# Attention and MLP layer: a weight scale for each half of w1, the first batch's MLP by halves of the weights, its first stage on four heads at a time, and its steps placed by times

## The chip, the cores and the metric

The kernel runs on one core of a Trainium2 chip. The metric is the device time of one execution in microseconds (us). A core has a matrix engine (TensorE, PE in the profile, with its weight loads as PEld), a vector engine (VectorE, DVE), an activation engine (ScalarE, ACT), a general engine (GpSimd, POOL) and a queue that issues the transfers (SyncE, SP). Each works through its own list of instructions in order and waits on semaphores for the others.

## The reference

Three pieces are computed in a row for 8 batches of 576 tokens and 512 columns (8 heads of 64).

```python
# stage 1: attention through a memory of 32 rows for each head
a = softmax(phi, axis=2)                       # [b, h, 576, 32]
k_m, v_m = a^T k, a^T v                        # [b, h, 32, 64]
x = softmax(q k_m^T / 8) v_m                   # heads side by side: [b, 576, 512]
# MLP with a mix over tokens of rank 32
u = x + ((x^T U) V)^T
y = u + relu(u @ w_ch1) @ w_ch2                # 512 -> 2048 -> 512
# stage 2: top 2 of 4 experts, each a causal attention with one head of 64
w = softmax over the two largest of y @ w_gate
out = sum over e of w_e * softmax(mask(q_e k_e^T / 8)) v_e @ wo[e]
```

The weights w_ch1, w_ch2, U and V come as float64, everything else as float32.

## The kernel before

**Numbers.** A float64 weight is read as two 32-bit words and turned into float32 by `conv64`: two passes on ACT, three on DVE (of which one, L337, takes the largest absolute value along), one addition on POOL. Then `split` writes it as two f16 parts, high and low, times a power of two that makes the largest value fit; the high part and, for some chunks, the scaled float32 are made on ACT, the low part on DVE (`L384`) or POOL (`L378`, `L380`). A matrix product is three f16 products: high by high, high by low, low by high.

**w1 and w2.** w1 is 8 chunks (`w1_load`, `w1_conv`, `w1_split`; 1 MB of words each, in 4 transfers of 256 KB), w2 too (`w2_load`, `w2_conv`, `w2_split`; 1 MB each). The words of w1 are put into the room of `w1s`, the tile that the f16 parts will have later; the float32 goes into the room of `w2s`. There is one scale for all of w1, so `w1_scale` needs all eight conversions, and the first split follows it. w2 has a scale for each chunk.

**MLP.** For each batch and each half of its tokens (288), `up` makes 16 tiles of 128 of the 2048 columns (12 matmuls of 128x288 each, `L999`), ACT and DVE make `h` of each (`L1003`, `L1005`), and `down` sums 8 of them into 4 tiles `dn` (24 matmuls, `L1015`), once for each half of the columns (`fg`). In the order of the program both halves `fg` of the first token half come before the second token half. `u_split` makes the f16 parts `uhl` of the input from `u` and its scale `us`.

**Stage 1** of a batch works on pairs of heads: `pair_kv` makes k_m and v_m (in the first batch in float32, with `L742`), `pair_kb` divides by the sums and puts the two heads apart (`own` is a mask), `pair_qT` transposes q (a transpose for one head, `L775`, and a matmul with the identity for the other, `L776`), `pair_scores`, `soft_a` and `soft_b` make the softmax, and for each half of the heads `half_p`, `half_t`, `half_tt`, `half_tx` and `half_u` make x and the token mix (tiles `at`, `tu`, `tt`, `tx`, `txs`, `u`). `u_max` and `u_scale` follow. Stage 2 (`y_`, `proj`, `vg`, `unit_`) of a batch and stage 1 of the next stand beside the MLP of the one between.

**Order.** Within an engine instructions run in the order in which they are traced, or as the tile scheduler reorders them. The set-up of the weights, batch 0's stage 1 and MLP and batch 1's stage 1 are traced in the order of a table, `ORDER`, written out step by step. From batch 1's MLP on, steps are taken from a heap by times in units of an `up` tile (`at`), and the last two stages follow a table `ORDER2`.

Of the kernel before, what the change touches and what calls it, by code (L numbers as in the profile page):

```python
# [46 lines left out]

ORDER = """  # L50
phi_load.0.0 phi_load.0.1 phi_max.0 phi_max.0 uv_load u_setup v_setup v_setup v_setup u_setup u_setup v_setup
phi_max.0 w1_load.0 w1_conv.0 w1_conv.0 phi_max.0 phi_max.0 raw_load.0.0.0 phi_sub.0.0 phi_sub.0.1 phi_sub.0.0 raw_load.0.0.1 v_setup w1_conv.0
w1_conv.0 phi_sub.0.1 pair_kv.0.0 w1_load.1 w1_load.2 w1_conv.1 w1_conv.1 w1_conv.1 pair_kb.0.0 raw_load.0.0.2
pair_qT.0.0 raw_load.0.1.0 raw_load.0.1.1 w1_conv.2 pair_kb.0.0 pair_kb.0.0 pair_kb.0.0 pair_qT.0.0 w1_conv.1
pair_kb.0.0 pair_kv.0.1 raw_load.0.1.2 raw_load.0.2.0 raw_load.0.2.1 u_setup pair_scores.0.0 w1_conv.0 w1_load.3
w1_load.4 pair_kb.0.1 pair_kb.0.1 pair_kb.0.1 pair_kb.0.1 pair_qT.0.1 pair_qT.0.1 pair_kb.0.1 soft_a.0.0 soft_a.0.0
w1_conv.2 w1_conv.2 pair_kv.0.2 pair_scores.0.1 raw_load.0.2.2 raw_load.0.3.0 pair_qT.0.2 raw_load.0.3.1
raw_load.0.3.2 pair_kv.0.3 soft_a.0.0 w1_conv.3 soft_b.0.0 soft_b.0.0 w2_load.0 w2_load.2 w1_conv.2 w1_conv.4
soft_b.0.0 soft_b.0.0 w1_conv.1 w1_conv.3 w1_load.5 w1_conv.3 pair_kb.0.2 pair_qT.0.2 pair_kb.0.2 pair_kb.0.2
w1_conv.2 w1_load.6 soft_a.0.1 pair_kb.0.2 soft_a.0.1 soft_a.0.1 pair_kb.0.2 v_setup w1_conv.4 pair_qT.0.3  # L60
pair_qT.0.3 soft_b.0.1 pair_kb.0.3 soft_b.0.1 pair_kb.0.3 w2_conv.0 soft_b.0.1 soft_b.0.1 pair_scores.0.2
pair_kb.0.3 pair_kb.0.3 half_p.0.0 w1_conv.3 pair_kb.0.3 soft_a.0.2 soft_a.0.2 soft_a.0.2 half_t.0.0 half_t.0.0
half_p.0.0 half_tt.0.0 w2_conv.0 half_tt.0.0 soft_b.0.2 w1_conv.4 half_tx.0.0 w2_conv.2 w1_conv.3 w1_load.7
soft_b.0.2 half_tx.0.0 soft_b.0.2 soft_b.0.2 w2_conv.0 half_tx.0.0 w2_conv.0 pair_scores.0.3 soft_a.0.3 half_tx.0.0
w1_conv.5 w2_conv.2 soft_a.0.3 soft_a.0.3 w2_conv.2 phi_load.1.0 half_u.0.0.0 half_u.0.0.0 w1_conv.6 soft_b.0.3
half_u.0.0.1 soft_b.0.3 soft_b.0.3 soft_b.0.3 half_p.0.1 half_u.0.0.1 w2_conv.2 w1_conv.4 w1_conv.5 w1_conv.7
half_t.0.1 half_p.0.1 half_tt.0.1 w1_conv.5 half_tt.0.1 half_tx.0.1 w1_conv.6 half_tx.0.1 phi_load.1.1 w1_conv.4
half_t.0.1 w1_conv.6 half_tx.0.1 w1_conv.5 w1_conv.7 w1_conv.7 half_tx.0.1 half_u.0.1.0 half_u.0.0.0 w1_scale
w1_conv.5 w2_conv.2 w2_conv.0 w2_conv.0 w1_conv.6 half_u.0.1.0 w2_load.4 w2_load.6 w2_conv.4 w1_scale w1_scale
half_u.0.1.0 w1_scale half_u.0.0.1 half_u.0.1.1 half_u.0.1.1 half_u.0.1.1 w1_conv.6 u_max.0 w1_split.0 w1_split.0  # L70
u_max.0 u_scale.0 w1_split.1 w1_split.2 w2_conv.2 w2_conv.0 w1_split.1 w1_split.1 u_scale.0 u_split.0.0 w2_conv.4
w2_conv.4 u_split.0.0 w1_split.3 w2_conv.4 w1_conv.7 w2_conv.0 w1_split.4 w1_split.5 w2_conv.2 w2_conv.2 up.0.0
w1_split.2 w2_split.0 w2_split.0 w2_conv.4 phi_max.1 up.0.0 up.0.0 w2_split.2 w2_conv.6 w2_split.2 up.0.1 up.0.2
up.0.1 up.0.1 w1_conv.7 w1_split.6 w2_conv.6 w2_conv.4 up.0.2 w1_split.7 up.0.2 w2_conv.6 up.0.3 up.0.4 up.0.5
up.0.3 w2_conv.4 up.0.3 w1_split.3 w1_split.4 w2_conv.4 w2_load.1 w1_split.3 u_scale.0 w2_conv.1 phi_max.1 up.0.4
up.0.4 phi_max.1 up.0.6 up.0.5 phi_max.1 w2_conv.6 up.0.5 w2_split.4 phi_max.1 phi_sub.1.0 up.0.6 w2_conv.1 w2_conv.1 w2_conv.6 up.0.7 up.0.7
up.0.6 up.0.7 phi_sub.1.0 w2_split.4 w2_load.3 w1_split.5 w2_conv.3 w2_conv.6 w2_conv.1 w2_conv.6 w2_conv.6
w1_split.6 w2_split.6 w2_conv.1 down.0.0.0.0 down.0.0.0.1 down.0.0.1.0 w2_conv.3 w2_conv.3 w2_load.5 phi_sub.1.1
phi_sub.1.1 w1_split.7 w2_conv.1 down.0.0.1.1 down.0.0.0.1 w2_conv.1 w2_conv.1 down.0.0.2.0 w2_split.1 phi_split.1.0
w2_conv.3 w2_split.1 w2_split.1 w2_conv.3 w2_split.6 down.0.0.2.1 down.0.0.3.0 down.0.0.2.1 w2_conv.3 down.0.0.1.1  # L80
phi_split.1.1 w2_conv.3 w2_conv.3 w1_split.5 w2_load.7 w2_conv.5 w2_conv.5 w2_conv.7 down.0.0.3.1 raw_load.1.0.0
down.0.0.3.1 w2_conv.5 up.0.8 up.0.8 up.0.9 up.0.10 up.0.8 w2_conv.7 w2_split.3 w1_split.7 up.0.9 up.0.9 up.0.10
up.0.10 w2_split.3 w2_conv.7 w2_conv.5 raw_load.1.0.1 raw_load.1.0.2 pair_max.1.0 pair_max.1.0 up.0.11 up.0.12
up.0.13 up.0.11 up.0.11 pair_scale.1.0 pair_scale.1.0 w2_conv.7 pair_scale.1.0 w2_conv.5 up.0.12 up.0.12 w2_conv.5
w2_conv.5 up.0.13 pair_hl.1.0.0 phi_split.1.1 up.0.13 up.0.14 up.0.15 up.0.14 up.0.14 w2_conv.7 w2_conv.7 up.0.15
# [1425 lines left out]
```

## Time and profile before

| what | value |
|---|---|
| runs, us | 1393.03 (median), 1390.7, 1398.51 |
| profiled execution, us | 1399.22 |
| its span, first to last instruction, us | 1397.2 |
| mean granted clock of TensorE | 0.970 |
| PE busy, us (share of the span) | 1270.1 (91%) |
| DVE busy | 969.3 (69%) |
| ACT busy | 787.4 (56%) |
| POOL busy | 405.8 (29%) |

An engine's busy time is the sum of its instructions' durations. The granted clock is the share of full speed at which the chip let TensorE run: 1.00 is 2.4 GHz, 0.50 is 1.2 GHz. The profiled execution is one more execution than the three timed ones.

### The profile page before, as it was taken

Reading aid. Unit: us, or ns where it says so; the run is one execution under the profiler, and the core shown is the slowest. Engines: PE = TensorE matmul, PEld = TensorE weight load, DVE = VectorE, ACT = ScalarE, POOL = GpSimd, SP = SyncE. Lnnn points to the kernel's source line nnn. Section 1 sums busy time; section 2 is a strip of 40 time slices with the busy share of each in tenths; the row PEclk is TensorE's granted clock in tenths of the full one; section 3 lists DMA queues with packets and bytes.
Section 4 is the critical chain, followed back from the end, with each engine's and each line's share of the span. In section 5 each row is a group of like instructions: output and inputs, shape, how many; then the busy total and the mean of one; then the engine's idle time right before and its main releaser. Section 6 shows DMA issues by size and latency. Waiting matters only on the chain. (4 is left out here: it accounts for less than half of the span.)

```text
span 1397.2 us, 31201 instructions
## 1 busy us (share of the span) xinstructions
PE 1270.1 (91%) x12021; PEld 973.9 (70%) x12021; DVE 969.3 (69%) x2669; ACT 787.4 (56%) x1888; POOL 405.8 (29%) x381
## 2 busy tenths in 40 slices
...
GB/s 286 206 91 30 132 89 33 10 65 86 95 69 44 83 64 77 70 52 93 76 73 56 80 64 78 70 48 91 75 69 41 95 65 53 57 13 33 42 81 110
DMA packets 253957, 106.42 MB, mean 76 GB/s; under 512 B 199056, under 2 KB 245328, under 8 KB 253808
## 3 DMA queue, kind: packets, MB, share of 16 engines
...
## 5 line engine op out<-in xcount | busy, mean ns | idle before, releaser
L999 PE MATMUL up<-uhl,w1s 128*128 128x288 f16 x3072 | 429.7, 293 | 40.1 <-DVE h L1005 34.8
L1015 PE MATMUL dn<-h,w2s 128*128 128x288 f16 x3072 | 409.9, 287 | 8.3 <-DVE h L1005 8.3
L999 PEld LDWEIGHTS <-w1s 128*128 128x128 f16 x3072 | 301.7, 100 | 133.5 <-issue 49.0
L1015 PEld LDWEIGHTS <-w2s 128*128 128x128 f16 x3072 | 295.0, 98 | 87.8 <-issue 11.7
L1237 POOL TENSOR_TENSOR phl<-pr,phl 128x128 f16<-128x128 f32 (+3 forms) x112 | 92.5, 826 | 331.0 <-ACT phl L1235 234.3
L1005 DVE SCALAR_TENSOR_TENSOR h<-up,h 128x288 f16<-128x288 f32 x256 | 113.0, 449 | 74.5 <-ACT h L1003 73.9
L1003 ACT ACTIVATE h<-up 128x288 f16<-128x288 f32 x256 | 100.8, 402 | 78.0 <-PE up L999 76.7
L1234 ACT ACTIVATE pr<-sc,nm 128x128 f32<-128x128 f32 (+3 forms) x112 | 58.7, 524 | 125.7 <-DVE nm L1228 69.8
L672 POOL TENSOR_TENSOR kvq<-raw,kvq 96x768 f16<-96x768 f32 x48 | 78.4, 1651 | 144.7 <-ACT raw L666 141.4
L633 DVE TENSOR_REDUCE amax<-raw 96x1 f32<-96x768 f32 x72 | 68.0, 946 | 67.8 <-DMA raw<-in_v_dram 31.2
L1022 DVE SCALAR_TENSOR_TENSOR u<-dn,us,u 128x288 f32<-128x288 f32 x128 | 65.3, 511 | 40.2 <-PE dn L1015 39.6
L1298 PEld LDWEIGHTS <-pT 128*128 128x128 f16 (+1 forms) x1260 | 56.2, 102 | 33.5 <-DMA pT<-phl 15.1
L1298 PE MATMUL av<-vhl,pT 128*128 128x64 f16 (+1 forms) x1260 | 68.0, 195 | 11.2 <-DMA pT<-phl 9.3
L1228 DVE CUSTOM_DVE_ANT_0 sc<-sc,wmask,ysc 128x128 f32<-128x128 f32 (+3 forms) x128 | 69.3, 550 | 12.1 <-PE sc L1225 11.1
L660 ACT ACTIVATE kvq<-raw,ps 96x768 f16<-96x768 f32 x72 | 62.6, 924 | 6.6 <-DVE ps L315 6.5
L1235 ACT ACTIVATE phl<-pr 128x128 f16<-128x128 f32 (+3 forms) x112 | 52.2, 466 | 13.9 <-DMA pT<-phl 12.0
L1334 ACT ACTIVATE ohl<-av,fac 128x64 f16<-128x64 f32 (+1 forms) x140 | 35.7, 307 | 41.1 <-PE av L1298 30.6
L1355 PE MATMUL wo<-wos,oT 128*128 128x512 f16 (+1 forms) x288 | 57.1, 348 | 1.2 <-ACT oT L1327 0.7
L1152 PE MATMUL vg<-wvg,yhl 128*128 128x260 f16 (+1 forms) x504 | 48.6, 256 | 0.0
L1104 PE MATMUL pj<-yhl,wqs 128*128 128x288 f16 x336 | 46.2, 286 | 0.7 <-ACT u L909 0.7
L1104 PE MATMUL pj<-yhl,wks 128*128 128x288 f16 x336 | 46.6, 286 | 0.0
L1119 ACT ACTIVATE qst<-pj 64x288 f16<-64x288 f32 x56 | 22.6, 404 | 40.6 <-PE pj L1104 40.1
...
## 6 DMA issues: line engine op xcount, KB each, us to landing
...
raw<-in_k_dram SPq DMA_DIRECT2D x48, 144.0 KB, 2.7
raw<-in_v_dram SPq DMA_DIRECT2D x48, 144.0 KB, 2.7
raw<-in_q_dram SPq DMA_DIRECT2D x48, 144.0 KB, 2.4
...
rx<-in_k_dram SPq DMA_DIRECT2D x16, 144.0 KB, 3.7
```

What stands on the lines that cost most here:

```text
L633: dve.tensor_reduce(o, raw, axis=AX.XYZ, op=ALU.max, apply_absolute_value=True)
L660: act.activation(hl[:, 0], src, AF.Copy, scale=s[0:SP, j:j + 1])
L672: pool.tensor_tensor(hl[:, 1], src, hl[:, 0], op=ALU.subtract)
L999: pe.matmul(pm, w1s[:, f // 2, a, kc, f % 2 * P:f % 2 * P + P], uhl[:, c, kc], start=(n == 0), stop=(n == 3 * KC - 1))
L1003: act.activation(hb[:, 0, g], pm, AF.Relu)
L1005: dve.scalar_tensor_tensor(hb[:, 1, g], pm, 0.0, hb[:, 0, g], op0=ALU.max, op1=ALU.subtract)
L1015: pe.matmul(pm, w2s[:, m, fg, a, g], hb[:, c, g], start=(g == 0 and a + c == 0), stop=(g == FG - 1 and a == 1))
L1022: dve.scalar_tensor_tensor(y, pm, st["us", b][:, 4 + KC * fg + m:5 + KC * fg + m], y, op0=ALU.mult, op1=ALU.add)
L1104: pe.matmul(pp[:, 0:NH], w[:, a, kc, ep * P:(ep + 1) * P], yhl[:, c, kc, ts_], start=(n == 0), stop=(n == 3 * KC - 1))
L1228: dve.tensor_tensor_reduce(psc[:, 0:n], psc[:, 0:n], wmask[:, (NT - 2 - i) * P:(NT - 1) * P], cs, 3.0e38, ALU.add, ALU.min, nm)
L1237: (dve if tail and TD >> (2*i + eo) & 1 else pool).tensor_tensor(phl[:, n:2 * n], pr[:, 0:n], phl[:, 0:n], op=ALU.subtract)
L1298: pe.matmul(pav[:n, eo * D:(eo + 1) * D], lhs, vhl[:kn, c, j, vs], start=(j == 0 and a + c == 0), stop=(j == i and a == 1))
```

## The change

The diff has four parts, shown here cut to their core.

First, w1 gets a scale for each half of its chunks, and the room for words and float32 is given out so that chunks 0 to 3 can be split before chunks 4 to 7 have been converted:

```diff
-    sw1 = cpool.tile([P, 2], F32, name="sw1")
+    sw1 = cpool.tile([P, 4], F32, name="sw1")
+    def slot(c):
+        return c if c < 4 else 2 + c % 2
+    def w1z(c):
+        return w2v[:, 2 * (c % 4) + c // 4]
     def w1_conv(c):
-        z = w2v[:, c]
-        yield from conv64(z, w1v[:, c % W1S].rearrange("p (n t) -> p n t", t=2), part[:, 0, c:c + 1], RP1 >> c & 1)
+        z = w1z(c)
+        yield from conv64(z, w1v[:, slot(c)].rearrange("p (n t) -> p n t", t=2), part[:, 0, c:c + 1], RP1 >> c & 1)
-    def w1_scale():
+    def w1_scale(g):
...
     def w1_split(c):
         yield from split(w1s[:, c, 0].rearrange("p k n -> p (k n)"), w1s[:, c, 1].rearrange("p k n -> p (k n)"),
-              w2v[:, c], sw1[:, 0:1], SP1 >> 2 * c & 3)
+              w1z(c), sw1[:, c // 4 * 2:c // 4 * 2 + 1], SP1 >> 2 * c & 3)
```

Second, batch 0's MLP goes through the first half of the columns for both token halves and then through the second; its `uhl` of the second token half gets tiles of its own:

```diff
-        for h_ in range(2):
-            for fg in range(2):
+        for x in range(4):
+            h_, fg = (x % 2, x // 2) if b == 0 else (x // 2, x % 2)
```

Third, `pair_kv` and `pair_kb` of batch 0 become steps on four heads, and q of batch 0 is loaded so that both heads of a pair lie side by side and are transposed together:

```diff
-                pe.matmul(pk[o:o + 64, n * P:n * P + (P if x is not None else 1)], e[:, c, 64 * p:64 * p + 64],
-                              x[:, :, c] if x is not None else one, start=(c == 0), stop=(c == C - 1))
+            for c in range(C):
+                for g in range(4):
+                    kv = st["rx", b, 2 * hf + g // 2][0:SP, 0:2]
+                    pe.matmul(pk[32 * g:32 * g + 32, 0:P], e[:, c, 4 * hf + g], kv[:, :, g % 2, c], start=(c == 0), stop=(c == C - 1))
...
-                pe.transpose(qp[c // R][0:64, t], raw[:, 0, c], ident[:SP, :SP])
-                pe.matmul(qp[c // R][64:128, t], raw[:, 1, c], ident[:SP, :SP], start=True, stop=True)
+                pe.transpose(qp[c // R][:, c % R * SP:c % R * SP + SP], raw[:, c].rearrange("p h d -> p (h d)"), ident[:SP, :SP])
...
+            for a in range(NA):
+                for h in range(2):
+                    nc.sync.dma_start(t[:, a * R:(a + 1) * R, h],
+                                      src[b, 2 * p + h, a * NH:(a + 1) * NH].rearrange("(p r) d -> p r d", r=R))
```

Fourth, the table `ORDER` goes, and its steps get times in the same heap as the later ones. Steps that only fill (`fill=True`) are pinned on DVE and ACT behind a main step of an earlier time:

```diff
+START, SLACK, SLACK2, LATER = 62, 2.5, 5, 5
...
+                for e in main:
+                    before_ = [i for t_, i in main[e] if t_ <= t - (SLACK if t < T0 else SLACK2) / UNIT]
+                    if pin and fill and before_:
+                        pins.enter_context(tc.issue_after(before_[-1]))
...
+    UNIT = 1.45
+    T0 = START / UNIT
+        at((10, 16, 22, 29)[c] / UNIT, w1_conv, c, fill=True)
+        at((42 + 2 * c) / UNIT, w1_split, c, fill=True)
+    at(38 / UNIT, w1_scale, 0, fill=True)
+    for n, (f, a) in enumerate(mlp(0)):
+        at(T0 + n, f, *a)
+        at(T0 + (4, 7, 11, 15)[c], w1_conv, 4 + c, fill=True)
+        at(T0 + 22 + 2 * c, w1_split, 4 + c, fill=True)
+    at(T0 + 20, w1_scale, 1, fill=True)
+    for t, f, a in stage1(1):
+        at(T0 + LATER + t, f, *a, fill=True)
+        at(T0 + 61 + w, sw_split, w, fill=True)
```

On DVE, shortly ahead of batch 0's first `up`, the program before has this (`w1mx` is the maximum over rows for w1's one scale, `sw_128` that scale, `um` and `ur` the maxima of `u` for the scale of `uhl`):

```order
L410 TENSOR_REDUCE part<-w1mx 128x1
L315 TENSOR_SCALAR sw_129<-t_117 128x1
L313 TENSOR_SCALAR sw_128<-part 128x1
L911 TENSOR_REDUCE um<-u_579 128x1
L317 TENSOR_SCALAR t_117<-t_117 128x1
L315 TENSOR_SCALAR sw_128<-sw_128 128x1
L317 TENSOR_SCALAR sw_128<-sw_128 128x1
L384 SCALAR_TENSOR_TENSOR w1s<-w2s,sw_128,w1s 128x1024 x4
L911 TENSOR_REDUCE um<-u_579 128x1
L915 TENSOR_REDUCE um<-um 128x1
L384 SCALAR_TENSOR_TENSOR w2s<-w2z_480,sw_129,w2s 128x1024
```

At the same place the changed program has this (its line numbers are its own: L320 stands for L384 of before, L242 for L306, L381 for L438, L820 and L828 for L857 and L865, L874 for L911, and on PE L992 for L999 and L1008 for L1015; `w2z` are w2's chunks in float32, `tt`, `ttf`, `th`, `txs` the token mix of the second half of batch 0's heads):

```order
L253 TENSOR_SCALAR t_117<-t_117 128x1
L320 SCALAR_TENSOR_TENSOR w1s<-w2s,sw_128,w1s 128x1024
L242 TENSOR_SCALAR dg<-identb,part 128x128
L874 TENSOR_REDUCE um<-u_539 128x1
L381 TENSOR_REDUCE mx<-w2mx_564 128x1
L874 TENSOR_REDUCE um<-u_539 128x1
L249 TENSOR_SCALAR t_117<-mx 128x1
L820 COPY tt<-tu_1_576 96x128
L251 TENSOR_SCALAR sw_129<-t_117 128x1
L320 SCALAR_TENSOR_TENSOR w1s<-w2s,sw_128,w1s 128x1024
L253 TENSOR_SCALAR t_117<-t_117 128x1
L828 TENSOR_TENSOR ttf<-tt_1_604,halves 128x64
```

The four splits of w1 on DVE in one row became two, apart from each other, with steps of stage 1 and of w2 between them; there are no conversions of w1 beyond chunk 3 above this place.

On PE, amid batch 0's MLP, the changed program has this between the tiles `dn_0_1_0` and `dn_0_1_1` (`tu`, `tt`, `tx` and `u` are the token mix of batch 1's first half of heads, `ar` and `w2mx` maxima for scales; 18 rows of `u` are left out):

```order
L1008 MATMUL dn_0_1_0_1877<-h_0_8_1554,w2s 128x288
L817 MATMUL tu_0_1538<-at,Uf 32x128 x6
L825 MATMUL tt_0_1552<-id_92,tt 128x32
L244 LDWEIGHTS onesb
L244 MATMUL ar_2_1573<-dg,onesb 128x3x96
L244 LDWEIGHTS onesb
L244 MATMUL w2mx_1578<-dg,onesb 128x128
L837 MATMUL tx_0_1587<-vtf,ttf 32x128 x2
...
L869 MATMUL u_1_0_1675<-V_113,txs 128x288
L869 MATMUL u_1_1_1676<-V_113,txs 128x288
L1008 LDWEIGHTS w2s
L1008 MATMUL dn_0_1_1_1915<-h_0_8_1554,w2s 128x288
```

Before, the same chain was spread: `tu`, `tt` and `tx` stand more than a hundred rows apart, and `tx`, for one, stands among `up` and `ss` (scores):

```order
L999 LDWEIGHTS w1s
L999 MATMUL up_1_9_2161<-uhl_1_1514,w1s 128x288
L874 MATMUL tx_0_1950<-vtf,ttf 32x128 x2
L719 LDWEIGHTS qT
L719 MATMUL ss_2_1999<-kb,qT 96x64
```

What moved is the rest of the MLP: in the changed program none of it stands between the steps of the chain.

On PE, at the end of batch 0's MLP, the program before has this (`u_2` and `u_3` are the second half of batch 1's heads; 20 more matmuls of `dn_1_1_3` follow before `ur`):

```order
L1015 LDWEIGHTS w2s
L1015 MATMUL dn_1_1_3_2459<-h_1_8_2147,w2s 128x288
L906 MATMUL u_2_0_2314<-V_113,txs 128x288
L906 MATMUL u_2_1_2315<-V_113,txs 128x288
L906 MATMUL u_3_0_2324<-V_113,txs 128x288
L901 LDWEIGHTS vth
L901 MATMUL u_3_1_2325<-aT,vth 128x288
L901 LDWEIGHTS vth
L901 MATMUL u_3_1_2325<-aT,vth 128x288
L906 MATMUL u_3_1_2325<-V_113,txs 128x288
L1015 LDWEIGHTS w2s
L1015 MATMUL dn_1_1_3_2459<-h_1_8_2147,w2s 128x288
```

The changed program has the whole chain of the second half behind the last row of `dn_1_1_3` (17 rows of `u` are left out):

```order
L1008 MATMUL dn_1_1_3_2407<-h_1_8_2071,w2s 128x288
L825 MATMUL tt_1_2187<-id_92,tt 128x32
L837 MATMUL tx_1_2208<-vtf,ttf 32x128 x2
...
L864 MATMUL u_3_1_2268<-aT,vth 128x288
L869 MATMUL u_3_1_2268<-V_113,txs 128x288
L244 LDWEIGHTS onesb
L244 MATMUL ur_2315<-dg,onesb 128x128
L244 LDWEIGHTS onesb
L244 MATMUL swmx_2376<-dg,onesb 128x384
L244 LDWEIGHTS onesb
L244 MATMUL swmx_2381<-dg,onesb 128x256
L992 LDWEIGHTS w1s
```

The `dn` rows that stood within and behind the chain now stand ahead of it. From the first `up` of batch 1 on, the two programs' rows are nearly the same.

## Rows read from the trace of the kernel before

**Rows 1.** Windows by stage; columns: busy us (instructions), granted clock, DMA, GB/s.
```profile
0.00:120.36 120.36, 75.34 (x352) 56.93 (x353) 88.70 (x155) 60.16 (x88) 55.73 (x46) 0.86 0.59 169
120.36:262.35 141.99, 120.82 (x1080) 92.88 (x1078) 111.06 (x248) 81.15 (x143) 50.78 (x32) 0.94 0.28 72
262.35:420.00 157.65, 153.56 (x1525) 119.09 (x1525) 117.58 (x331) 91.70 (x228) 47.50 (x46) 0.99 0.31 70
```

**Rows 2.** DVE's groups by form, 0 to 120.36 us.
```profile
L343 DVE SCALAR_TENSOR_TENSOR w2s<-w1s,w2s 128x1024 uint32<-128x1024 uint32 x8 | 11.8, 1475 | 0.0
L337 DVE TENSOR_SCALAR_CACHE_REDUCE w2s<-w2s 128x1024 f32<-128x1024 f32 x8 | 9.7, 1208 | 0.1
L384 DVE SCALAR_TENSOR_TENSOR w1s<-w2s,sw,w1s 128x1024 f16<-128x1024 f32 x4 | 9.6, 2437 | 2.1 <-ACT w1s L382 2.1
L343 DVE SCALAR_TENSOR_TENSOR w2z<-w2r,w2z 128x1024 uint32<-128x1024 uint32 x4 | 8.9, 2216 | 0.0
L339 DVE TENSOR_SCALAR w2s<-w2s 128x1024 uint32<-128x1024 uint32 x8 | 8.2, 1019 | 0.1
```

**Rows 3.** PE's groups by form, 0 to 120.36 us.
```profile
L742 PE MATMUL kv<-rx,e 96*64 96x128 f32 x96 | 21.7, 422 | 4.5 <-ACT e L587 4.5
L776 PE MATMUL qt<-ident,rx 96*64 96x96 f32 x48 | 14.0, 394 | 0.0
...
L775 PE MATMUL qt<-ident,rx 96*64 96x96 f32 x24 | 8.9, 369 | 0.0
...
L742 PE MATMUL kv<-one,e 96*64 96x1 f32 x48 | 5.5, 242 | 0.0
...
L794 PE MATMUL at<-ident,at 96*128 96x96 f32 x12 | 2.4, 376 | 0.0
L854 PE MATMUL tu<-at,Uf 96*32 96x128 f32 x24 | 2.2, 421 | 3.1 <-POOL at L829 3.1
```

**Rows 4.** Waits, 0 to 120.36 us: total us, times, longest.
```profile
ACT qT L780 <- PE qt L776: 22.7, 8, 5.7
...
DVE iv L751 <- PE kv L742: 14.6, 2, 7.7
```

**Rows 5.** Timeline about batch 0's first up (start, us; in brackets idle before).
```profile
119.82 1.21 DVE L343 SCALAR_TENSOR_TENSOR w2z<-w2r,w2z 128x1024 uint32<-128x1024 uint32 x1
...
121.08 1.40 DVE L975 SCALAR_TENSOR_TENSOR uhl<-u,us,uhl 128x1152 f16<-128x1152 f32 x1
...
122.53 7.13 PE L999 MATMUL up<-uhl,w1s 128*128 128x288 f16 x33 [1.25 <-DVE uhl L975]
...
136.08 1.63 PE L999 MATMUL up<-uhl,w1s 128*128 128x288 f16 x12 [1.30 <-DVE sw L315]
```

**Rows 6.** Windows of 10 us (columns as in group 1).
```profile
100.00:110.00 10.00, 0.96 (x3) 0.48 (x2) 7.89 (x5) 9.90 (x11) 7.69 (x4) 0.50 0.00 0
120.00:130.00 10.00, 8.75 (x43) 5.60 (x44) 9.57 (x19) 6.17 (x9) 3.56 (x1) 0.57 0.14 45
130.00:140.00 10.00, 6.35 (x50) 4.67 (x49) 9.93 (x11) 7.79 (x14) 9.41 (x4) 1.00 0.17 60
170.00:180.00 10.00, 5.45 (x32) 3.57 (x31) 9.28 (x14) 7.61 (x13) 5.01 (x4) 0.83 0.54 116
```

**Rows 7.** Timeline ahead of batch 1's first up.
```profile
250.89 0.41 PE L874 MATMUL tx<-vtf,ttf 128*32 128x128 f32 x4
...
251.98 4.21 PE L1015 MATMUL dn<-h,w2s 128*128 128x288 f16 x33
...
256.82 2.75 PE L1015 MATMUL dn<-h,w2s 128*128 128x288 f16 x21
...
262.35 0.53 PE L999 MATMUL up<-uhl,w1s 128*128 128x288 f16 x3 [0.72 <-ACT uhl L973]
```

**Rows 8.** DMA issues of the span: count, KB, median us to landing.
```profile
raw<-in_q_dram SPq DMA_DIRECT2D x48, 144.0 KB, 2.4
...
sw<-in_moe_wq_dram SPq DMA_DIRECT2D x4, 128.0 KB, 2.9
```

More of the change, by code (lines that the diff above doesn't have):

```diff
@@ L39 @@
 SP2 = 1028
-W1S = 4
 RB = 3
@@ L55 @@
[L55 to L59, printed above, removed]
@@ L75 @@
[L75 to L79, printed above, removed]
@@ L80 @@
[L80 to L84, printed above, removed]
@@ L948, in stage1 @@
                 hf = p // 2
-                add(t0 + 10.4, half_t if b else half_t_first, hf)
+                add(t0 + 10.4, half_t, hf)
                 add(t0 + 10.5, half_p, hf)
```

298 lines of the change are left out of this document (157 added, 141 removed).

## The prediction

> **What bounds the kernel now.** I read the stretches first. The page puts PE busy for 91% of the span, but that is an average over two different kernels. From batch 1's first `up` tile on, PE works 153.56 of 157.65 us [rows 1] and nothing in the change can win much there. Before it lie two stretches that are not full: the set-up with batch 0's stage 1 (0 to 120.36 us, PE 75.34, DVE 88.70), and batch 0's MLP beside batch 1's stage 1 (141.99 us, PE 120.82, so 21 us idle). The change touches these two alone. In the order of instructions, everything from batch 1's first `up` tile on stands almost as it stood; so the time moves by as much as that tile moves, now at 262.35 us [rows 7].
>
> The first stretch is a stretch of DVE: PE does almost nothing from 100 to 110 us (0.96 us busy) while DVE has 7.89 and ACT 9.90 [rows 6]. The groups of DVE [rows 2] show what it does: conversions of the double-word weights and their splits. The first `up` needs chunk 0 of w1 alone, but its scale needs all eight. The waits add that DVE stood 14.6 us for the `kv` matmuls of stage 1, and ACT 22.7 for `qt` [rows 4].
>
> **The change, part by part.**
>
> *1. A scale for each half of w1.* One w1 chunk costs DVE 1.208 + 1.019 + 1.475 = 3.70 us [rows 2]. Four chunks leave the stretch: -14.8 us. So do two of its four DVE splits: 2 x 2.437 = -4.9. Two more splits of w2 come in ahead, at some 1.3 us each (the 1.40 us of `uhl`'s low half, 1152 columns [rows 5], scaled to 1024 columns: 1.25): +2.6. The low half of `uhl`, now ahead: +1.4 [rows 5]. Two more w2 scales and the wider `kb` steps are short instructions that no group shows; I set them at +1.5 and -0.8. DVE ahead of the first `up`: 88.7 - 14.8 - 4.9 + 2.6 + 1.5 + 1.4 - 0.8 = 74 us.
>
> *2. Stage 1 on four heads at a time.* `kv` is 96 matmuls with 64 output rows in 21.7 us, 0.226 each (and 48 for the sums, 5.5) [rows 3]. After the change they are 96 of 32 rows, each head against its own 128 columns of k and v, and 24 for the sums. The nearest form with 32 rows, `tu`, takes 2.2 us for 24, 0.09 each: 8.7 + 2.7 = 11.4 us where 27.2 stood (if the 0.226 holds, 24). `qt` is 72 instructions of 22.9 us [rows 3] and becomes 24 transposes, which at the 0.2 us of `at` (2.4 us for 12) make 5. These are 34 us of PE work less, in a stretch in which PE is not full: it counts only where someone waits, DVE's 14.6 us [rows 4] above all. I take that as gone.
>
> *3. When does the first `up` start?* DVE is idle 120.36 - 88.7 = 31.7 us before. Without the 14.6 that is 17, and 74 + 17 = 91. GpSimd's share also falls (four conversions and four splits fewer), and with it the stretching of DVE: the same L343 takes 2.216 us on average [rows 2], and 1.21 when nothing runs beside it [rows 5]. Some 3 us of that come back: 88. Bounds: 78, if DVE idles no more than 4 us; 100, if DVE's share stays at 88.7/120.36 = 74%, as 74/0.74.
>
> A rule speaks against it. q of batch 0 comes in 16 loads of 256-byte pieces instead of 8 with longer ones. The whole trace has 128 KB in 256-byte pieces (`sw` of wq) landing in 2.9 us, and 144 KB of q in 2.4 [rows 8]: 1.36 times as long per byte. By these rows 1.18 MB of q cost 1.18/0.128 x 2.9 - 1.18/0.144 x 2.4 = 7 us of landing, laid over each other, and so 2 at most on the path; it is inside the 78 to 100. The Trainium skill (DMA: Bandwidth & Descriptors, Specifications) wants pieces of at least 512 bytes for the line rate; by it these loads would count about double, an estimate of 4 us of a full queue at the 169/0.59 = 286 GB/s of a busy queue [rows 1]. The trace agrees in direction, by 1.36 and not by 2.
>
> *4. Batch 0's MLP by halves of the weights.* What left the first stretch comes back here. DVE: 111.06 + 14.8 + 3.5 (two splits, at less contention than before) - 4 (one and a half w2 conversions, done earlier) - 2.6 (two w2 splits) - 1.4 (`uhl`) - 5.3 (the splits of `sw`, now behind batch 1's first `uhl`) - 1.5 = 115 us; ACT rises too, from 81.15 of 141.99. PE keeps its 121. The first two quarters are `up` and `down` of both token halves with chunks 0 to 3, so the chunks 4 to 7 have two quarters, some 2 x 33 us (16 items of 1.63 us each [rows 5], and a share of the idle time), to be loaded, converted and split. The table of times puts the last conversion 15 and the last split 28 steps of 1.45 us behind the MLP's start, 22 and 41 us; with a conversion and a split of delay (3.7 + 2.4) the last chunk is ready at 47. `up` 8 comes after 32 items, at about 66. Hidden by PE's two quarters, with 19 us to spare; beyond that each us late is a us lost.
>
> PE's idle time here is what decides. (a) 8 us as before, spread (of the 21 before, those in the windows 120 to 140 and 170 to 180 [rows 6] are about half). (b) 3 us at the start (the first `up` waits for the low half of `uhl`, 1.25 before [rows 5]). (c) In the order, batch 1's chain for its first half of heads (`tu`, `tt`, `tx`, `u`) stands back to back between two `dn` tiles, where before `dn` matmuls were spread among them. Its bare latencies are about 5 us; DVE has conversions of 1.0 to 2.2 us between its steps, so I take 12 (5 to 20). (d) At the end the same chain of the second half stands behind the last `dn`. Before, it ran from 250.89 (`tx`) to 262.35 with 33 and 21 `dn` matmuls, 4.21 + 2.75 us, in its gaps [rows 7]. Without these PE has 2 to 3 us of work in 12.5 (the 11.46 and a us from `tt` to `tx`): 10 idle. Sum: 121 + 8 + 3 + 12 + 10 = 154 us against 141.99. Bounds: 142 (the pockets are filled by moving everything else up) and 170 (DVE at 115/170 = 68%, less than in either stretch).
>
> *5. The splits of `sw`* stand on DVE and ACT between batch 1's first `uhl` and its first `h`: four on DVE of 1.25 us (as above), 5 us, of which the `up` tiles already free to run cover most: +2 (0 to 5).
>
> **Sum.** Batch 1's first `up` at 88 + 154 + 2 = 244, against 262.35: 18 us. The profiled execution took 1399.22 us; its like would take 1381. The median of the runs is 6.2 us lower than that execution, so 1393.03 - 18 = 1375.
>
> **The rivals.** *A: the second stretch grows not at all.* For: PE idles 21 us in it and DVE is at 78%; 115 us of DVE at 78% make 147. Against: the order of (c) and (d). With 142, a first `up` at 84, and 2 for the `sw` splits it gives 228: 34 us, 1359.
>
> *B: the gain is given back.* The first `up` comes at 100 since DVE's share stays 74%, and the second stretch takes 160 because the second half of w1 is late: the margin of 19 us goes if each of the four conversions and splits takes half as long again beside `h` and `u` on DVE (9.28 to 9.93 of 10 us busy at 120 to 140 and at 170 to 180 [rows 6]). 100 + 160 + 2 = 262: no change, 1393.
>
> *C: slower, by the clock.* PE's granted clock is 0.50 of full from 100 to 110 and still 0.57 from 120 to 130, with PE 8.75 us busy there: after the idle stretch it worked a while at the lower level, 1.2 GHz. The pockets (c) and (d) could each bring that. 25 us of PE work in each following piece at half speed cost 12.5 more: 88 + 154 + 2 + 25 = 269, 1400. It decides from there: about 25 us beyond the forecast's sum. For it: 0.83 at 170 to 180 with PE 5.45 busy. Against: at 130 to 140 PE has 6.35 busy and the clock is 1.00 [rows 6], so such pockets alone need not lower it.
>
> *D: the change doesn't do what it says* on `kv`: if the 32-column matmuls cost 0.226 each, PE keeps 13 us and DVE half of its 14.6 us wait; the first `up` at 95, 1382, inside the forecast's own range.
>
> **How the numbers follow.** A measurement of this kernel can tell about 0.5%, 7 us, from no change. Forecast (gain of 8 to 30 us, D in it): 0.60. A: 0.15. B: 0.14. C: 0.11. Faster is forecast and A: 0.75; same is B: 0.14; slower is C: 0.11. The time is that of the forecast, 1375, its own range 1363 to 1386: 6 us to either side for the first `up`, and 5 or 6 for the two pockets. The range for 8 in 10 reaches 1353 (A with 78 for the first `up`: 78 + 142 + 2 = 222, 40 us) to 1397 (B and a little); what is left out is C and small parts of A and B.
>
> **What would show it.** In the profile after: the first `up` near 88 us, with four conversions of w1 ahead of it; DVE's wait for `kv` gone, and the 32-column `kv` near 0.09 us; PE idle in one pocket amid `dn_0_1` and one after the last `dn` of batch 0, about 10 us each; batch 1's first `up` near 244; nothing moved behind it by more than 2 us. I am wrong if the first `up` comes after 100, if `up` 8 of the first token half waits for w1, if the clock is at its lower level beyond the first `up` for more than 20 us, or if the stretches behind batch 1's first `up` change.

## The result

The changed kernel took 1379.32 us (median of 4 runs, 1378.6 to 1382.06), the kernel before 1395.77 (4 runs, 1390.7 to 1400.68): a ratio of 0.9886, 95% interval 0.9843 to 0.9929. In a later set of runs it took 1378.04 (4 runs) beside 1390.92 (13 runs): 0.9896, 0.9859 to 0.9934. So it is faster by about 1%, 13 to 16 us. 1375 had been predicted, and the range of 1353 to 1397 holds the time.

The windows by stage, of the changed kernel, cut at the first `up` of batch 0 and of batch 1 (against [rows 1]):

```profile
0.00:88.19 88.19, 43.07 (x277) 33.14 (x278) 65.52 (x142) 48.34 (x77) 37.96 (x37) 0.89 0.71 204
88.19:238.67 150.48, 125.26 (x1077) 95.36 (x1076) 120.13 (x249) 87.50 (x148) 63.95 (x38) 0.89 0.32 84
238.67:396.30 157.63, 151.40 (x1489) 117.00 (x1489) 122.62 (x340) 94.97 (x230) 44.98 (x45) 0.98 0.33 70
```

The first `up` came at 88.19 us (120.36 before, 88 predicted), batch 1's at 238.67 (262.35 before, 244 predicted). What lies behind it took 1376.7 - 238.67 = 1138.0 us of the span, 1134.9 before. So the traces say 23.7 us won and 3.2 given back; but a second trace of the changed kernel has 1141.1 us behind that point, so 3 us there is what one kernel differs by from execution to execution. The runs say 13 to 16 in all, since the profiled execution of before (1399.22 us) was one of its slower ones and that of the changed kernel (1378.6) its fastest.

DVE's groups of the first stretch (against [rows 2]; L279 is L343 of before, L320 is L384, L275 is L339):

```profile
L279 DVE SCALAR_TENSOR_TENSOR w2z<-w2r,w2z 128x1024 uint32<-128x1024 uint32 x4 | 5.0, 1256 | 0.0
...
L279 DVE SCALAR_TENSOR_TENSOR w2s<-w1s,w2s 128x1024 uint32<-128x1024 uint32 x4 | 4.9, 1223 | 0.0
...
L320 DVE SCALAR_TENSOR_TENSOR w1s<-w2s,sw,w1s 128x1024 f16<-128x1024 f32 x2 | 2.9, 1464 | 0.4 <-ACT w1s L318 0.4
L275 DVE TENSOR_SCALAR w2s<-w2s 128x1024 uint32<-128x1024 uint32 x4 | 2.9, 722 | 0.1
```

An L279 on w2's chunks takes 1.256 us where it took 2.216, a split of w1 1.464 where it took 2.437. PE's groups of the same stretch (against [rows 3]):

```profile
L695 PE MATMUL kv<-rx,e 96*32 96x128 f32 x96 | 6.8, 419 | 9.4 <-DMA rx<-in_v_dram 7.0 <-ACT e L539 2.3
L698 PE MATMUL kv<-one,e 96*128 96x1 f32 x24 | 5.4, 354 | 0.0
...
L739 PE MATMUL qt<-ident,rx 96*128 96x96 f32 x24 | 4.7, 373 | 0.0
```

96 `kv` matmuls with 32 rows take 6.8 us, 0.071 each (0.226 before, 0.09 estimated). The 24 for the sums take 5.4, 0.225 each: twice what I took, and no less than the 48 of before (5.5). The 24 transposes of q take 4.7. `kv` now waits 7.0 us for loads of v, which it did not before.

### The profile page after: what moved, and what is told of

It reads as the page before. It is cut to its first block, busy times and chain, and to the rows that moved or that the text cites. A ratio compares the mean times of both kernels' runs of the same rounds, so it can differ in the third digit from the quotient of the medians.

```text
span 1376.7 us, 31068 instructions
## 1 busy us (share of the span) xinstructions
PE 1241.8 (90%) x11948; PEld 952.8 (69%) x11948; DVE 964.3 (70%) x2671; ACT 786.8 (57%) x1886; POOL 401.7 (29%) x379
## 5 line engine op out<-in xcount | busy, mean ns | idle before, releaser
L992 PE MATMUL up<-uhl,w1s 128*128 128x288 f16 x3072 | 425.1, 291 | 35.6 <-DVE h L998 30.3
L1008 PE MATMUL dn<-h,w2s 128*128 128x288 f16 x3072 | 416.4, 289 | 4.7 <-DVE h L998 4.1
L992 PEld LDWEIGHTS <-w1s 128*128 128x128 f16 x3072 | 299.3, 99 | 125.8 <-issue 44.5
L1008 PEld LDWEIGHTS <-w2s 128*128 128x128 f16 x3072 | 297.0, 99 | 89.6 <-issue 8.5
L1015 DVE SCALAR_TENSOR_TENSOR u<-dn,us,u 128x288 f32<-128x288 f32 x128 | 64.9, 509 | 33.3 <-PE dn L1008 32.7
L1292 PEld LDWEIGHTS <-pT 128*128 128x128 f16 (+1 forms) x1260 | 56.3, 102 | 41.3 <-DMA pT<-phl 23.7
L1113 ACT ACTIVATE qst<-pj 64x288 f16<-64x288 f32 x56 | 22.7, 406 | 42.1 <-PE pj L1098 41.7
```

What stands on the lines that cost most here:

```text
L992: pe.matmul(pm, w1s[:, f // 2, a, kc, f % 2 * P:f % 2 * P + P], uhl[c][:, kc], start=(n == 0), stop=(n == 3 * KC - 1))
L1008: pe.matmul(pm, w2s[:, m, fg, a, g], hb[:, c, g], start=(g == 0 and a + c == 0), stop=(g == FG - 1 and a == 1))
L1015: dve.scalar_tensor_tensor(y, pm, st["us", b][:, 4 + KC * fg + m:5 + KC * fg + m], y, op0=ALU.mult, op1=ALU.add)
L1292: pe.matmul(pav[:n, eo * D:(eo + 1) * D], lhs, vhl[:kn, c, j, vs], start=(j == 0 and a + c == 0), stop=(j == i and a == 1))
```

## The experiments

All differ from the changed kernel by the edit shown, except the ninth row, which differs from the kernel before. In the table stand the median and number of runs, the ratio to the kernel before with its interval, and from the trace the end of batch 0's last `u` matmul, the first `up` of batch 0 and of batch 1, and DVE's busy time up to the latter (us). Each ratio is to runs of the kernel before in the same set; its median was 1395.77, 1392.28, 1393.48 and 1390.92 in the four sets (changed; one scale to q in pairs; times only to no pins; the rest), so times of different sets are comparable to some 5 us.

| run | time (runs) | ratio | last `u` | first `up` | batch 1's | DVE busy |
|---|---|---|---|---|---|---|
| before | - | 1 | 100.95 | 120.36 | 262.35 | 199.75 |
| changed | 1379.32 (4) | 0.9886 (0.9843 to 0.9929) | 82.34 | 88.19 | 238.67 | 185.65 |
| changed, again | 1378.04 (4) | 0.9896 (0.9859 to 0.9934) | 82.82 | 88.62 | 239.05 | 183.59 |
| one scale | 1381.0 (5) | 0.9929 (0.9901 to 0.9957) | 70.99 | 89.88 | 238.31 | 182.08 |
| tokens first | 1389.84 (10) | 0.999 (0.9964 to 1.0015) | 86.23 | 96.19 | 248.91 | 190.26 |
| `kv` in pairs | 1391.47 (10) | 1.0001 (0.997 to 1.0033) | 90.20 | 96.06 | 248.58 | 188.96 |
| q in pairs | 1396.9 (9) | 1.0039 (1.0019 to 1.006) | 88.46 | 94.32 | 246.05 | 189.79 |
| times only | 1387.45 (10) | 0.9963 (0.9933 to 0.9993) | 82.14 | 101.05 | 248.11 | 186.12 |
| table, four heads | 1396.96 (10) | 1.0012 (0.9978 to 1.0046) | 87.96 | 107.03 | 255.35 | 201.65 |
| w2 later | 1382.74 (10) | 0.9917 (0.989 to 0.9944) | 66.20 | 78.8 | 238.82 | 185.38 |
| no pins | 1401.17 (10) | 1.0062 (1.0038 to 1.0086) | 103.94 | 115.19 | 263.96 | 190.33 |
| LATER 2 | 1393.48 (10) | 1.0006 (0.9982 to 1.003) | 83.52 | 91.81 | 258.11 | 187.62 |
| LATER 0 | 1375.01 (4) | 0.987 (0.9833 to 0.9908) | 84.56 | 92.89 | 240.19 | 183.76 |
| LATER 0, `sw` early | 1377.57 (4) | 0.9891 (0.9857 to 0.9924) | 83.66 | 92.0 | 240.34 | 183.61 |

**One scale for w1.**

```diff
-        dve.tensor_reduce(part[:, 0, o:o + 1], part[:, 0, 4 * g:4 * g + 4], ...)
+        dve.tensor_reduce(part[:, 0, o:o + 1], part[:, 0, 0:NC1], ...)
-        at(T0 + (4, 7, 11, 15)[c], w1_conv, 4 + c, fill=True)
+        at((35, 39, 44, 49)[c] / UNIT, w1_conv, 4 + c, fill=True)
-    at(38 / UNIT, w1_scale, 0, fill=True)
+    at(55 / UNIT, w1_scale, 0, fill=True)
-        at((36, 40, 46, 54)[c] / UNIT, w2_conv, 2 * c, fill=True)
+        at((52, 56, 62, 70)[c] / UNIT, w2_conv, 2 * c, fill=True)
```

> The changed kernel, but with one scale for all of w1 again: all eight conversions and the maximum over them come ahead of the first split; the order by halves, the steps on four heads and the times stay (the MLP's start is put 16 us later in the table). Theory 1 (DVE's queue sets the first `up`, and the halves take four conversions and two splits out of it): 4 x 3.3 us of conversions and some 5 us of ACT and DVE behind the scale come back, so the first `up` at 105 to 110 us instead of 88.19; the second stretch gets shorter by about half of it, since DVE and PE there had idle time that the conversions filled: 140 to 146 instead of 150.5; in all 8 to 14 us slower than the changed kernel, about 1390. Theory 2 (the gain comes from stage 1 on four heads): the first `up` stays under 95 and the time within 4 us of 1379.

Theory 1's numbers did not come: with all eight conversions ahead the first `up` came 1.7 us later, not 17 to 22, and batch 1's not later at all. Theory 2's did (89.88, and 1381.0 us). But the edit had to move w2's conversions back too, and so is two edits: DVE's busy time ahead of the first `up` is 68.98 us for 65.52, so this run alone does not refute that DVE's sum sets it. The timeline shows what that did: `u`, `uhl` and `up` of batch 0.

```profile
69.80 1.19 PE L869 MATMUL u<-V,txs 96*128 96x288 f32 x4 [0.22 <-ACT txs L850]
...
88.58 2.39 ACT L966 ACTIVATE uhl<-u,us 128x1152 f16<-128x1152 f32 x2
...
89.88 0.88 PE L992 MATMUL up<-uhl,w1s 128*128 128x288 f16 x3 [6.04 <-ACT uhl L966]
```

Stage 1's last `u` ended at 70.99, 11 us earlier than in the changed kernel, as w2's work no longer stood among its steps; then `uhl` started only 17.6 us later, behind w1's scale and splits and conversions of w2 in the queues of DVE and ACT. This led to theory 3: the first stretch ends with stage 1's own chain, and each part of the weights' work delays it where it stands ahead in a queue.

**Tokens first.**

```diff
-            h_, fg = (x % 2, x // 2) if b == 0 else (x // 2, x % 2)
+            h_, fg = x // 2, x % 2
-        at(T0 + (4, 7, 11, 15)[c], w1_conv, 4 + c, fill=True)
+        at(T0 + (-8, -5, -1, 3)[c], w1_conv, 4 + c, fill=True)
```

(and the second half's loads, scale and splits, and w2's odd chunks, earlier likewise)

> The changed kernel, but batch 0's MLP goes through both halves of the columns for the first token half, then for the second, as before; the scale for each half stays, and the second half's conversions, splits and w2's odd chunks are put 12 to 16 items earlier. Theory 1 (two quarters of cover are what hides the second half of w1): `up` 8 is wanted about 26 us earlier, the splits of chunks 4 to 7 were ready 11 to 16 us before they were wanted, so PE waits 8 to 15 us for w1 ahead of `up` 8 or for w2's odd chunks ahead of the second `dn`, and some conversions move ahead of the first `up` (at 90 to 95); batch 1's first `up` 10 to 15 us later than 238.67, the time 1388 to 1395. Theory 2 (the order by halves is not needed, the conversions fit into one quarter): batch 1's first `up` within 3 us, the time within 4 us of 1379.

The times came as theory 1 said (batch 1's `up` 10.2 us later, the time 10.5), by the second of its two ways: three conversions moved ahead of the first `up`, which came 8 us later; the second stretch grew by 2.2. `up` 8 itself did not wait for w1. So the order by halves is worth about 10 us here, as the room into which conversions go.

**`kv` in pairs** puts `pair_kv` and `pair_kb` of the kernel before back, **q in pairs** its loads and `pair_qT`:

```diff
-                add((15.5, 24)[hf], half_kv_first, hf)
-                add((20, 29)[hf], half_kb_first, hf)
+                    add((15.5, 16.7, 24, 25.5)[2 * hf + pp], pair_kv_first, 2 * hf + pp)
+                    add((20, 21.5, 29, 31)[2 * hf + pp], pair_kb_first, 2 * hf + pp)
```

> The changed kernel, but `kv` and `kb` of batch 0 on pairs of heads with 64 output rows, as before; the transposes of q and the loads stay as changed. Theory 1: PE gets 27 us of such matmuls instead of 12, the maximum over DVE's wait of 14.6 us comes back in part: the first `up` 4 to 12 us later than 88.19, the second stretch as it was, the time 1383 to 1391. Theory 2 (PE has room there and DVE's queue of conversions covers the wait): the first `up` within 2 us, the time within 3 us of 1379.

```diff
-                pe.transpose(qp[c // R][:, c % R * SP:c % R * SP + SP], raw[:, c].rearrange("p h d -> p (h d)"), ident[:SP, :SP])
+                pe.transpose(qp[c // R][0:64, t], raw[:, 0, c], ident[:SP, :SP])
+                pe.matmul(qp[c // R][64:128, t], raw[:, 1, c], ident[:SP, :SP], start=True, stop=True)
```

> The changed kernel, but q of batch 0 in two loads of a pair with longer pieces, and transposed by a transpose and a matmul for each head, as before; `kv` stays on four heads. Theory 1: PE gets 23 us of such work instead of 5, in a stretch in which it then has about 61 of 88 us busy; ACT's wait for qt (22.7 us before) comes back, and the first `up` is 2 to 8 us later, the time 1381 to 1387. Theory 2 (the pieces of 256 bytes cost more than the transposes give): the first `up` is earlier by 1 to 4 us. Theory 3: neither matters, within 1 us.

On the first `up` theory 1 holds for both: the last `u` ends 7.9 and 6.1 us later, and the first `up` moves by just as much, as a chain does. The times came out above it, 1391.47 just beyond 1383 to 1391 and 1396.9 well beyond 1381 to 1387. Nor did the waits come back as it said: with `kv` on pairs DVE waits 4.7 us for it (2.8 in the changed kernel, 14.6 before), and with q in pairs ACT waits 10.6 for `qt` (22.7 before). In the second, PE's groups show the price of the old form (L739 of the changed kernel took 4.7):

```profile
L732 PE MATMUL qt<-ident,rx 96*64 96x96 f32 x48 | 13.9, 394 | 0.0
L731 PE MATMUL qt<-ident,rx 96*64 96x96 f32 x24 | 8.8, 369 | 2.8 <-DMA rx<-in_q_dram 2.8
```

The 256-byte pieces of q are no loss against that; what they cost by themselves is not shown, since the edit undoes both. (With q in pairs `kv` does not wait for v, but it also starts later.) Of the 17.6 us by which q in pairs was slower, 7.4 lie ahead of batch 1's first `up`; and 1145.9 us of its trace lie behind it (1138.1 and 1141.1 in the two of the changed kernel); where that goes I did not find.

**Times only** undoes one scale, `kv` and q at once; **table, four heads** puts the new steps of stage 1 into the kernel before:

```diff
-pair_kv.0.0 ... pair_kv.0.1 ... pair_kb.0.0 ... pair_kb.0.1
+half_kv.0.0 ... half_kb.0.0 pair_scores.0.0
```

> The changed kernel with three of its parts undone at once: one scale for w1, `kv` and `kb` on pairs of heads, q loaded and transposed as before. What is left of the change are the times in place of the table and the order of batch 0's MLP by halves. Theory 3, formed after the first four runs (the stretch ends with stage 1's own chain, which runs late by what stands ahead of its steps in the queues of PE, DVE and ACT): the delays of the three add, the first `up` at 89.9 + 7.9 + 6.1 = 104 us, batch 1's first `up` at 255 to 257, so most of the 32 us on the first `up` is the three parts and about half of it the times; the time 1398 to 1410. Theory 1 as it stood (DVE's sum alone): the first `up` at 90 to 93 like with one scale.

> The kernel before, its table kept, with `kv` and `kb` on four heads and q of batch 0 as changed (each step at the place where the pair's second step stood). Theory 3: stage 1's matmuls of `u` end earlier than 100.95 us by up to 14 us, but in the table the eight splits of w1 stand on ACT and DVE ahead of the last steps of stage 1 (the copy of `u`, its maximum `um`, `us`) and these 16 us stay, since the splits wait for the eighth conversion; the first `up` at 108 to 118, the time 1382 to 1391. Rival (the four-head steps are the gain): the first `up` at 100 to 106, the time under 1382.

Both gave a first `up` near theory 3's (101.05 for 104; 107.03 just under the 108 to 118), and both times missed it: 1387.45 lies 10 us under the 1398 to 1410, 1396.96 6 us over the 1382 to 1391. So the prices of the parts do not add: undone one at a time, one scale, `kv` and q cost about 2, 12 and 18 us by the medians (5, 15 and 20 by the ratios), and all three at once 8 (10). What is left then, the times and the order by halves, is still 0.1 to 0.7% faster than before. A likely reason, not tested, is the table of times: for times only, as for one scale, the MLP's start was put 16 us later, while the two on pairs kept times made for shorter steps. What one of these runs costs is then the part in that table, not the part alone.

Four heads in the old table brought the first `up` 13.3 us forward, the 14 of the two runs above; the remaining 18.8 us to 88.19 need the rest of the change. This run is the clearest on theory 3: the last `u` ends 13 us earlier than before, and the first `up` still comes 19.1 us after it (19.4 before), with the same row of splits ahead of the maximum:

```profile
90.09 8.31 DVE L322 SCALAR_TENSOR_TENSOR w1s<-w2s,sw,w1s 128x1024 f16<-128x1024 f32 x3 [1.09 <-ACT w1s L320]
...
98.32 0.74 DVE L869 TENSOR_REDUCE um<-u 128x1 f32<-128x576 f32 x1
...
107.03 0.93 PE L961 MATMUL up<-uhl,w1s 128*128 128x288 f16 x3
```

DVE's busy time ahead of the first `up` is 90.97 us, 88.70 before: DVE's sum would have put it later, not 13 us earlier. With the old table batch 1's first `up` came 7 us earlier in the trace and the median time did not change, so the four-head steps alone won nothing that the runs show.

**W2 later.**

```diff
-        at((36, 40, 46, 54)[c] / UNIT, w2_conv, 2 * c, fill=True)
-        at((50, 53, 56, 61)[c] / UNIT, w2_split, 2 * c, fill=True)
+        at((50, 54, 58, 64)[c] / UNIT, w2_conv, 2 * c, fill=True)
+        at((64, 67, 70, 74)[c] / UNIT, w2_split, 2 * c, fill=True)
```

> The changed kernel with the loads, conversions and splits of w2's even chunks put 10 to 14 us later in the table of times, so that they stand behind stage 1's last steps rather than among them; nothing else. Theory 3: with one scale (first run) stage 1's last `u` matmul ended at 71 us where w2's conversions had been moved back, against 82.3 in the changed kernel; so the first `up` comes at 77 to 82 us instead of 88.2; the second stretch gets two conversions more (some 8 us of DVE) and grows by 2 to 8: batch 1's first `up` at 230 to 238, the time 1371 to 1379. Theory 1 (DVE's sum): the first `up` earlier by the 2 x 3.2 us of conversions that leave, 80 to 83. Rival (the first `down` waits for w2): the first `up` as early, but batch 1's no earlier than 238.

The timeline of the same three steps:

```profile
65.29 0.91 PE L869 MATMUL u<-V,txs 96*128 96x288 f32 x4
...
77.51 2.39 ACT L966 ACTIVATE uhl<-u,us 128x1152 f16<-128x1152 f32 x2
...
78.80 0.88 PE L992 MATMUL up<-uhl,w1s 128*128 128x288 f16 x3 [3.45 <-ACT uhl L966]
```

Theory 3 is right on the first `up` (78.8; theory 1's 80 to 83 is close to it), and, beside the first run, this gives a price for the scale for each half: with w2 moved back in both (by a few us differently), 78.8 against 89.88, some 11 us. But batch 1's first `up` stayed at 238.82, and the time was not better: the second stretch took 160 us for 150.5. That is the rival's number; its reason is not seen, as the first `dn` tiles waited 1.84 us for a scale of w2 and no more. The windows show what stood there instead (DVE's busy time is the number behind PE's and PEld's):

```profile
60.00:80.00 20.00, 6.89 (x24) 4.35 (x25) 19.46 (x34) 16.37 (x26) 12.87 (x6) 0.63 0.36 97
80.00:100.00 20.00, 15.91 (x111) 11.57 (x111) 19.69 (x33) 15.29 (x26) 7.61 (x4) 0.86 0.43 130
100.00:130.00 30.00, 21.53 (x158) 16.07 (x156) 28.21 (x45) 20.60 (x30) 19.76 (x9) 0.89 0.35 97
```

DVE works 67.4 of the 70 us from 60 to 130, 59.1 in the changed kernel. What left the first stretch stands in DVE's queue of the next, and `up` 8 of the first token half began at 148.97, in the changed kernel at 150.36: of the 9.4 us won, 8 were gone by then.

**No pins.**

```diff
-    run(True)
+    run()
```

> The changed kernel without the pins: steps that fill may be scheduled ahead of main steps on DVE and ACT. Theory 3: conversions and splits then stand ahead of stage 1's steps (in the order DVE has 25 instructions more ahead of the low half of `uhl`), and the first `up` comes 8 to 20 us later, the time 1385 to 1400. Rival (the scheduler finds as good an order): within 3 us of 1379.

The first `up` came 27 us later, more than I expected, and the time was 22 us longer. The weights' work then stands ahead of stage 1's steps again: the last `u` ends at 103.94, for 82.34, and DVE is busy 95.50 us ahead of the first `up`, for 65.52.

**LATER 2, LATER 0, and `sw` early.**

```diff
-START, SLACK, SLACK2, LATER = 62, 2.5, 5, 5
+START, SLACK, SLACK2, LATER = 62, 2.5, 5, 0
```

> The changed kernel once more, unaltered, beside the three that follow on the same chip, since the runs of before spread from 1384 to 1408 us and those of the changed kernel have been four. Both theories: 1378 to 1384, batch 1's first `up` at 237 to 240 us.

> The changed kernel with batch 1's stage 1 three units (4.4 us) earlier in the table of times (LATER 2 for 5). In its order on PE the last chain (`tt`, `tx`, `u`, `ur`) then stands among `up` 15 and the `dn` tiles of the last quarter instead of behind them; the first chain stays between `dn_0_1_0` and `dn_0_1_1`. Theory 3 (the two pockets on PE are a cost of where the chains stand): the pocket of 6 us ahead of batch 1's first `up` goes to 2 or less, the one at 170 to 190 us stays; batch 1's first `up` at 232 to 236, the time 3 to 6 us under the changed kernel's. Rival (DVE is full, so that what goes earlier there delays `h`): no earlier than 237.

> The same with LATER 0 for 5 (7.3 us earlier). Now the first chain too stands among `up` 8 to 14 of the third quarter. Theory 3: both pockets go (some 11 us idle at 170 to 200 and the lower clock behind it, 4 to 5 us, and 6 at the end; before's stretch had 21 idle): batch 1's first `up` at 222 to 230, the time 8 to 14 us under the changed kernel's. Rival (DVE at 60 to 130 us has over 90% busy when the first `up` comes early, and batch 1's stage 1 adds to it): the gain at the end is lost ahead of it, batch 1's first `up` at 234 to 240.

> LATER 0 and the steps of stage 2's weights (`sw_load`, `sw_max`, `sw_scale`, `sw_split`) 8 units earlier. In the order `swmx` and the splits still stand about batch 1's first `uhl`, but ahead of more of its `h`. Theory 3: some of the 4 us by which batch 1's MLP was longer than before (151.2 against 147.2 from one `ur` to the next) come back: 1 to 3 us under LATER 0 alone. Rival: the loads of 2 MB then meet those of w2 and k, v, q, and nothing or 1 to 3 us is lost.

LATER 2 was no better but 19 us later on batch 1's first `up` and 15 us slower, with PE waiting for w2's splits (6.1 us), for `u` of the MLP on DVE (7.9) and for `kv`'s operands (4.3). The rival's number came; its reason, a full DVE, is not shown, as DVE was busy 73% of that time. LATER 0 did spread both chains, and batch 1's first `up` came at 240.19, not at 222 to 230 (the rival said 234 to 240). Its timeline on PE has the idle time elsewhere: ahead of `dn` for w2's splits, and little at the end.

```profile
189.41 0.66 PE L1008 MATMUL dn<-h,w2s 128*128 128x288 f16 x2 [5.07 <-ACT w2s L318]
...
193.63 5.10 PE L1008 MATMUL dn<-h,w2s 128*128 128x288 f16 x22 [2.53 <-DVE w2s L320]
...
237.79 0.34 PE L244 MATMUL swmx<-dg,onesb 128*128 128x384 bf16 x1 [1.24 <-DVE dg L242]
```

PE was idle for 25.3 us of that stretch, 25.2 in the changed kernel. So the two pockets are not what sets the end; theory 3's half on them falls. `sw` early brought nothing over LATER 0, as its rival said. LATER 0 is 3 us under the changed kernel, with ranges that overlap (1373.88 to 1376.63, and 1374.82 to 1382.07): no version clearly better was found.

## Why the prediction came out right

*The first `up` at 88.* The number was right and the reason was not. I added DVE's work (74 us, less 3 for shorter instructions) and its idle time (17); measured were 65.5 and 22.7, two errors that cancelled by luck. What ends the stretch is stage 1's chain. In the kernel before (PE's last `u`, DVE's splits, the last of ACT's, the copy of `u`, its maximum, `uhl`):

```profile
100.10 0.85 PE L906 MATMUL u<-V,txs 96*128 96x288 f32 x1
...
103.41 8.31 DVE L384 SCALAR_TENSOR_TENSOR w1s<-w2s,sw,w1s 128x1024 f16<-128x1024 f32 x3 [1.08 <-ACT w1s L382]
...
107.43 1.13 ACT L373 ACTIVATE w1s<-w2s,sw 128x1024 f16<-128x1024 f32 x1
108.47 0.39 ACT L909 ACTIVATE u<-u 128x288 f32<-128x288 f32 x1
...
111.64 0.74 DVE L911 TENSOR_REDUCE um<-u 128x1 f32<-128x576 f32 x1
...
117.18 1.25 ACT L973 ACTIVATE uhl<-u,us 128x1152 f16<-128x1152 f32 x1 [2.24 <-DVE us L315]
```

The matmuls end at 100.95, then the copy on ACT stands behind splits of w1 until 108.47, the maximum on DVE behind 8.31 us of splits until 111.64; the first `up` comes 19.4 us after the last `u`. After:

```profile
81.65 0.69 PE L869 MATMUL u<-V,txs 96*128 96x288 f32 x1
82.37 0.41 ACT L872 ACTIVATE u<-u 128x288 f32<-128x288 f32 x1 [0.62 <-PE u L869]
...
82.81 0.75 DVE L874 TENSOR_REDUCE um<-u 128x1 f32<-128x576 f32 x1 [1.48 <-ACT u L872]
...
86.88 2.40 ACT L966 ACTIVATE uhl<-u,us 128x1152 f16<-128x1152 f32 x2 [2.02 <-DVE us L251]
...
88.19 0.88 PE L992 MATMUL up<-uhl,w1s 128*128 128x288 f16 x3 [1.79 <-ACT uhl L966]
```

Now it comes 5.85 us after the last `u`. Of the 32.2 us won on the first `up`, 18.6 are an earlier end of stage 1's matmuls, and 13.6 a shorter tail. The table of before ends with the splits in one row, which I showed and read as DVE's work, not as work that stood ahead of a chain.

*`kv` and q.* The sum held, 16.9 us where 16.4 were estimated (50.1 before), with the `kv` products below their estimate and the sums at twice theirs. DVE's wait for `kv` did go, from 14.6 to 2.8 us; but that it is what they shorten was only partly so, as on pairs it came back to 4.7 and the whole chain moved, by 7.9 and 6.1.

*The scale for each half* I took as DVE's 20 us. It is worth some 11 us on the first `up` where w2 is out of the way, and in the one run without it nothing on batch 1's.

*The second stretch, 154 us:* 150.5. The pockets were where the order showed them. Windows of 10 us:

```profile
168.00:178.00 10.00, 4.68 (x37) 2.80 (x35) 7.83 (x20) 8.33 (x13) 4.61 (x3) 0.81 0.16 30
178.00:188.00 10.00, 5.63 (x52) 3.90 (x50) 9.60 (x9) 4.81 (x8) 6.85 (x4) 0.84 0.53 128
188.00:198.00 10.00, 7.93 (x60) 5.64 (x58) 6.99 (x24) 6.87 (x13) 4.53 (x4) 0.50 0.94 202
228.00:238.67 10.67, 4.55 (x24) 2.39 (x22) 8.81 (x28) 4.22 (x9) 0.00 (x0) 0.70 0.15 28
```

From 168 to 188 PE was idle for 9.7 us (12 estimated) and in the last window for 6.1 (10 estimated). The first pocket's causes were others than I named: the transposing transfer of `aT`, and a short instruction of DVE (0.25 us elsewhere) that took 1.97 beside POOL:

```profile
175.89 0.66 PE L864 MATMUL u<-aT,vth 128*128 128x288 f16 x2 [4.57 <-DMA aT<-ah]
...
184.76 2.37 POOL L281 TENSOR_TENSOR w2z<-w2z,w2r 128x1024 int32<-128x1024 int32 x1 [1.22 <-issue]
185.22 1.97 DVE L242 TENSOR_SCALAR dg<-identb,part 128x128 bf16<-128x128 bf16 x1
...
187.24 0.22 PE L244 MATMUL w2mx<-dg,onesb 128*128 128x128 bf16 x1 [3.93 <-DVE dg L242]
```

Rival C appeared in small: the clock is 0.50 from 188 to 198, behind the pocket, and PE's busy time of the stretch is 125.3 us, not 121. Over the whole stretch the mean clock is 0.89, 0.94 before [rows 1]: by these means some 33 us at the lower level for 17, in pieces. Added up, that is over the 20 us which the prediction named as a sign of being wrong; it goes with 4 us more of PE's time than before, not with 25. The end of the stretch, with `tx`, `ur` and the first `up`:

```profile
229.02 0.41 PE L837 MATMUL tx<-vtf,ttf 128*32 128x128 f32 x4 [0.69 <-DVE ttf L828]
...
235.66 0.29 PE L244 MATMUL ur<-dg,onesb 128*128 128x128 bf16 x1 [1.86 <-DVE dg L242]
...
238.67 0.88 PE L992 MATMUL up<-uhl,w1s 128*128 128x288 f16 x3 [0.63 <-ACT uhl L966]
```

The second half of w1 was hidden, as forecast: its last split on DVE ended at 141.45, on POOL at 146.8; `up` 8 of the first token half began at 150.36. But that is 59 and 62 us behind the first `up`, where 47 and 66 were estimated: some 3 us to spare, not 19.

*The sum* treated the two stretches as two terms, 88 and 154. The runs show that they are not independent: with a first `up` between 78.8 and 92.9, batch 1's came at 238.3 to 240.3 in five kernels (one of them traced twice). What ties them is open. One account is DVE's queue, which was nearly full behind the first `up` in w2 later. It is not shown: DVE was busy 76 to 78% of the time up to batch 1's first `up` in these kernels and in the kernel before alike, and 72 to 79% in all others, so its share does not single them out; and no run changes DVE's work alone. DVE's time up to there fell from 199.75 to 185.65 us, but that is no measure of less work: 9.2 of these 14.1 us stand behind batch 1's first `up` instead (778.7 us from there to the end, 769.5 before), the splits of `sw` with 5.1 among them, as estimated. In the whole span DVE's busy time is 964.3 us for 969.3. The kernels at 72 and 73% (no pins, LATER 2) show that an order can also be worse than this.

*The time* was to move by as much as batch 1's first `up`. In the traces that tile came 5 us earlier than the 244, and yet the median is 4 us above the 1375. With executions of one kernel that spread over some 3 to 20 us, and one or two traces of each, the runs cannot tell whether the later stages gave something back.

*The 2 us for `sw`'s splits:* batch 1's MLP took 151.9 us from one maximum `ur` to the next, 147.6 before, so 4.3 were given back. That the splits are the cause is not shown: with LATER 0 it took 150.5, with `sw` early besides 152.6.
